# A transformer block on one core: the first feed-forward product by Strassen's seven half-sized products, one segment's output projection moved beside the feed-forward part, and phi finished on VectorE

## The chip, the cores and the metric

The kernel runs on 1 core of one Trainium2 chip. The metric is device time in microseconds (us), lower is better; a time is the median of several runs. TensorE (PE) does matrix products, VectorE (DVE) and ScalarE (ACT) elementwise work, GpSimd (POOL) selections and some elementwise work, and SyncE (SP) issues nearly every DMA.

## The reference

One block over 2048 tokens of 512 channels in float32: a modulated layernorm, an attention with a running memory in four segments of 512 tokens and 32 heads of 16 channels, an output projection, a second modulated layernorm, and a feed-forward part with squared ReLU.

```
phi = lambda t: where(t > 0, t + 1.0, exp(t))
for s in range(4):                                  # segments of 512 tokens
    a_dot = softmax(qs @ ks.T * scale + mask) @ vs
    a_mem = (phi(qs) @ M) / (phi(qs) @ z + 1e-6)
    o_s = g * a_mem + (1 - g) * a_dot
    M += phi(ks).T @ vs;  z += phi(ks).sum()
h = layernorm(x) * (1 + ca) + sa;   x = x + ga * (attention(h) @ wo)
h = layernorm(x) * (1 + cb) + sb;   x = x + gb * (relu(h @ w1 + b1)**2 @ w2 + b2)
```

Here w1 is 512 x 1792 and w2 is 1792 x 512. The change concerns `h @ w1`, phi, the two layernorms' reciprocal root, and the place of one quarter of `attention(h) @ wo`.

## The kernel before

**Precision.** Each large product is made of three float32r products: both operands are split into a high part and the rest, by a copy on ACT (high) and a subtraction on DVE or POOL (low), and high*high, high*low and low*high are added up in PSUM. So every operand of a product costs one ACT and one DVE or POOL instruction, and every product three matmuls.

**Attention.** It works in units: one unit is 8 heads of one segment (16 units, `u`). For a unit `qk` projects q and k channel-major into two PSUM banks, and L817 and L819 split them into `sg`, which DMAs (L835) scatter into the slots of `ST`. `a_quad` makes raw scores to find row maxima (L893, with DVE at L898), `b_quad` makes them again with the maximum subtracted (L1053), ACT takes the exponential (L1070), POOL zeroes the upper triangle (L1057), and L1112 multiplies by v (`bpv`). phi is built from the same banks: exp on ACT (L824), relu on ACT (L826), min(exp, 1) on POOL (L828) and the sum on POOL (L829). `heads_out` stores the raw result to DRAM, loads back denominators (L1171, L1173), forms the gates on DVE, stores and loads them spread out (L1192, L1195), multiplies on POOL (L1198) and stores the turned result (L1213).

**Output projection and second layernorm.** `wo_tile(g)` handles 128 tokens: load and split the attention result, 12 matmuls (L1244 to L1246, `bwop`), add x and take layernorm statistics on DVE. `ln2(s)` takes the reciprocal root for a segment in 11 small DVE instructions (L625 to L630), normalizes (L633), transposes on TensorE (L642, `blnq`), applies the modulation and splits the result into `H2a` (segments 0, 2) or the space of `WVO` (1, 3).

**Feed-forward part.** 14 slices `f` of 128 hidden channels. Weights are loaded and split once, while segment 0 is worked on, and stay. `ffn1(s, f)` makes 4 x 3 matmuls of 128x128 weights by 512 tokens (L1405 to L1407, `bh`). ACT adds the bias and clips (L1415) and squares into the high part (L1419), DVE squares again (L1422) and subtracts (L1423). `ffn2(s, f, t)` adds three matmuls (L1433 to L1435) to the output bank of each of the four 128-token tiles (`bpf`).

**What sets the order.** Every step is an `op` with an engine, an assumed duration, its predecessors, and the pool slots and PSUM banks it takes and gives back. A planner (`Plan.run`) walks the five engines in assumed time. On each engine it takes the steps in the order that the table `ORDER` lists by number, and emits them in that order. On the chip each engine is then a strict queue in that order; a step that must wait holds up everything behind it. The memory of the attention part (`sb`) is closed and given to the feed-forward weights at `open_ffn`; a tile there waits for the last use of what lay in its place.

## Time and profile before

| | |
|---|---|
| median of 3 runs | 799.09 us (796.88 to 800.13) |
| the profiled execution: its time | 797.94 us |
| the profiled execution: its span | 796.2 us |
| mean granted TensorE clock | 0.980 |
| instructions | 15771 |

The span runs from the first to the last instruction; 1.7 us of the execution's time lie around it. Roughly, the attention part lasts until 435 us, a change-over until 467 us, and the feed-forward part until the end. Busy shares add up the instructions' own times; matmuls are pipelined, so the distance between the starts of two neighbours, not their length, tells what one costs.

### The profile page before, as it was taken

How to read it: one execution, taken by the hardware profiler on the slowest of the kernel's cores; microseconds unless marked ns; L12 is line 12 of the kernel's file. 1: busy time of each engine (PE TensorE's matmuls, PEld its weight loads, DVE VectorE, ACT ScalarE, POOL GpSimd, SP SyncE). 2: the span in 40 equal slices, each digit the busy share in tenths (PEclk: the TensorE clock that was granted, in tenths of full speed). 3: DMA queues.
4: the chain of work that ended last, by engine and by line, in shares of the span. 5: the costliest groups of instructions: out<-in, count | busy, mean ns of one | idle time of the engine just before them, and what ended most of it. 6: DMA issues, size and time to landing. Idle time of an engine off the chain costs nothing.

```text
span 796.2 us, 15771 instructions
## 1 busy us (share of the span) xinstructions
PE 761.8 (96%) x5623; PEld 568.0 (71%) x5627; DVE 502.4 (63%) x1353; ACT 439.5 (55%) x931; POOL 277.4 (35%) x362
## 2 busy tenths in 40 slices
...
GB/s 258 199 152 95 239 186 175 116 126 159 194 174 167 168 196 165 174 154 194 201 224 220 109 216 118 93 67 27 0 1 1 1 76 4 1 0 80 1 0 54
DMA packets 76568, 95.29 MB, mean 120 GB/s; under 512 B 17349, under 2 KB 36553, under 8 KB 76490
## 3 DMA queue, kind: packets, MB, share of 16 engines
...
q8 instruction: 45, 0.74, 0.4%
...
q10 hardware_dynamic: 152, 0.13, 0.0%
...
## 4 chain that ended last, share of the span: by engine, by line
PE 73%; DMA 7%; ACT 6%; DVE 5%; SPq 5%; POOL 2%; issue 2%; ACTq 0%; DVEq 0%; POOLq 0%
PE bh L1407 7%; PE bh L1405 7%; PE bh L1406 7%; PE bpf L1434 7%; PE bpf L1433 6%; PE bpf L1435 6%; PE bpv L1112 6%; PE bqk L780 5%; PE bv L860 4%; PE bpb L1053 4%; PE ba L893 4%; ACT pt L1070 3%; SPq L835 3%; PE blnq L642 2%; PE bwarm L546 2%
## 5 line engine op out<-in xcount | busy, mean ns | idle before, releaser
L898 DVE CUSTOM_DVE_ANT_0 ba<-ba,msk 128x128 f32<-128x128 f32 (+2 forms) x384 | 186.5, 543 | 57.2 <-PE ba L893 44.6
L1070 ACT ACTIVATE pt<-bpb 128x512 f32<-128x512 f32 x320 | 171.5, 615 | 19.6 <-PE bpb L1053 17.2
L1422 DVE TENSOR_TENSOR r<-r 128x512 f32<-128x512 f32 x56 | 38.7, 692 | 136.8 <-ACT rr L1419 136.6
L780 PE MATMUL bqk<-HT,WQK 64*128 64x512 f32 x720 | 101.9, 399 | 0.2 <-POOL hinge_s L510 0.2
L1415 ACT ACTIVATE r<-bh,b1c 128x512 f32<-128x512 f32 x56 | 38.6, 689 | 109.5 <-PE bh L1407 65.0
L1057 POOL TENSOR_SCALAR_AFFINE_SELECT pt<-pt 128x512 f32<-128x512 f32 x128 | 79.9, 644 | 39.7 <-ACT pt L1070 31.8
L1434 PE MATMUL bpf<-W,rr 128*128 128x512 f32 x224 | 88.1, 393 | 0.0
L1433 PE MATMUL bpf<-W,rr 128*128 128x512 f32 x224 | 88.1, 393 | 0.0
L1435 PE MATMUL bpf<-W,rr 128*128 128x512 f32 x224 | 87.6, 391 | 0.0
L1112 PE MATMUL bpv<-pt,VT 128*32 128x512 f32 (+3 forms) x1024 | 81.5, 446 | 3.7 <-DVE mx L898 2.9
L1053 PE MATMUL bpb<-ST 64*128 64x256 f32 (+2 forms) x512 | 80.3, 353 | 3.1 <-ACT ac L931 1.2
L893 PE MATMUL ba<-ST 63*128 63x256 f32 (+2 forms) x512 | 78.0, 351 | 1.6 <-ACT phi L826 0.7
L780 PEld LDWEIGHTS bqk<-HT,WQK 64*128 64x128 f32 x720 | 71.6, 187 | 10.2 <-POOL hinge_s L510 0.9
L1419 ACT ACTIVATE rr<-r 128x512 fp32r<-128x512 f32 x56 | 35.4, 632 | 69.9 <-PE bpf L1435 65.7
L1053 PEld LDWEIGHTS bpb<-ST 64*128 64x128 f32 x512 | 51.1, 185 | 26.3 <-ACT pt L1070 6.7
L893 PEld LDWEIGHTS ba<-ST 63*128 63x128 f32 x512 | 51.7, 186 | 25.1 <-ACT pt L1070 7.3
L1198 POOL TENSOR_TENSOR X1L<-X1L 128x512 f32<-128x512 f32 x40 | 51.6, 1294 | 20.8 <-DMA X1L<-o_gate 18.9
L1112 PEld LDWEIGHTS bpv<-pt,VT 128*32 128x32 f32 x1024 | 29.1, 110 | 37.9 <-issue 26.4
L898 DVE DVE_READ_ACCUMULATOR2_ANT mx<- 128x1 f32 x384 | 54.1, 141 | 0.1
L860 PE MATMUL bv<-WVO,HT 64*128 64x512 f32 x384 | 53.8, 395 | 0.0
L1405 PE MATMUL bh<-H2a,W 128*128 128x512 f32 x112 | 45.5, 406 | 6.3 <-ACT W L1373 6.3
L1433 PEld LDWEIGHTS bpf<-W,rr 128*128 128x128 f32 x224 | 42.1, 188 | 9.8
(157 smaller groups left out, 1433.7 us busy)
## 6 DMA issues: line engine op xcount, KB each, us to landing
...
```

The costliest lines, as they stand in the source:

```text
L780: m = nc.tensor.matmul(bank(("qk", u, w)), W3(w, k, x, cc * P, (cc + 1) * P)[z], HT[z, y, k], start=(ph == 0 and k == 0 and i == 0), stop= ...
L860: m = nc.tensor.matmul(bank(("v", s, t)), HT[z, x, k, t * P:(t + 1) * P], WVO[z, k, y], start=(ph == 0 and k == 0 and i == 0), stop=(ph == ...
L893: nc.tensor.matmul(dst[:, c0:c0 + n], ST[b:b + 63, 0, sl, qt * P:(qt + 1) * P], ST[b:b + 63, 1, sl, :n], start=True, stop=True)
L898: nc.vector.tensor_tensor_reduce(i, i, msk[:, 512 - n:], scale=1.0, scalar=-3e38, op0=ALU.add, op1=ALU.max, accum_out=o)
L1053: nc.tensor.matmul(dst, ST[b:b + 64, 1, sl, kb * P:(kb + 1) * P], ST[b:b + 64, 0, sl, q0:512], start=True, stop=True)
L1057: nc.gpsimd.affine_select(out=ap, in_=ap, pattern=[[0, ap.shape[1]], [1, P]], compare_op=ALU.is_ge, fill=0.0, base=0, channel_multiplier=-1)
L1070: ns = [act(512, lambda j=j: nc.scalar.activation(buf("PPP"[n], pt)[:, i + j], bank(keys[j]), AF.Exp, scale=0.25), pr[slot] + 0.01 + 0.001 ...
L1112: nc.tensor.matmul(bank(o)[32 * hq:32 * hq + 32, q0:q0 + src.shape[1]], v[:, a:a + 32], src, start=start, stop=stop, tile_position=(0, 32 ...
L1405: nc.tensor.matmul(p, wh, h2[:, 0, k], start=(k == 0), stop=False)
L1433: nc.tensor.matmul(p, rh, FF["W2"][:, f, 0], start=(f == 0), stop=False)
L1434: nc.tensor.matmul(p, rh, FF["W2"][:, f, 1], start=False, stop=False)
L1435: nc.tensor.matmul(p, rl, FF["W2"][:, f, 0], start=False, stop=(f == NF - 1))
```

## The change

**ffn1.** The token axis of a segment is cut in two halves of 256, the contraction in two halves of 2 x 128 channels, and the hidden channels in pairs of slices (`q`, seven per segment). A 2x2 block product then needs 8 half-sized products; a Strassen-type scheme needs seven. `ln2` forms seven combinations of the normalized activations (four subtractions) and splits each; `load_w1` forms seven combinations of the weights (four additions) and splits them. Per pair `q`, TensorE makes 7 products of 2 x 3 matmuls, each 256 wide, into two banks (`bhx`, `bhy`), and DVE adds them up into the four blocks of the hidden layer (L1504, L1507). Then ACT clips twice, squares, and copies the high part, all four blocks together, and DVE subtracts (L1533). The combined weights of all slices don't fit, so `load_w1(s, q)` loads and combines them again for every segment, in two buffers. Sums x1 of segments 0 to 2 are kept in DRAM (`x1_dram`) and loaded back.

**Output projection.** `wo_tile` of segment 2 joins segment 3's beside the feed-forward part; its low parts go from POOL to DVE.

**phi.** ACT's relu and POOL's sum become one DVE instruction that takes max(., 0) of the PSUM bank and adds min(exp, 1).

**Layernorm.** The reciprocal root becomes two POOL instructions, an addition and a power. In the first layernorm of segments 1 to 3, half of the modulation goes from ACT to DVE.

`ORDER` is another table. Its effect at three places follows. TensorE around the last score-times-value product (`bpv`, the end of attention), before:

```order
L1246 MATMUL bwop<-WVO,oT 128x512
L1112 MATMUL bpv<-pt,VT_139 32x512 x4
L1112 MATMUL bpv<-pt,VT_139 32x384 x4
L1112 MATMUL bpv<-pt,VT_139 32x128 x4
L1112 MATMUL bpv<-pt,VT_139 32x256 x4
L642 MATMUL blnq<-ident,xh 128x128 x8
L1244 MATMUL bwop<-WVO,oT 128x512
```

and changed:

```order
L650 MATMUL blnq<-ident,x_6398 128x128 x4
L650 MATMUL blnq<-ident,x_6453 128x128 x4
L650 MATMUL blnq<-ident,x_6902 128x128 x4
L650 MATMUL blnq<-ident,x_6664 128x128 x4
L1119 MATMUL bpv<-pt,VT_142 32x512 x4
L1119 MATMUL bpv<-pt,VT_142 32x384 x4
L1119 MATMUL bpv<-pt,VT_142 32x128 x4
L1119 MATMUL bpv<-pt,VT_142 32x256 x4
L1260 MATMUL bwop<-WVO,oT 128x512
```

All transposes of segment 0's second layernorm now stand ahead of the last `bpv`. Behind it stood 16 transposes and 36 matmuls of `bwop` before the first `bh`; now 21 of `bwop` stand there before the first `bhx`: the rest of segment 1's last tile and nine matmuls of segment 2's first. Ahead of it stand 84 matmuls of `bwop`, where there were 108.

SP at the same place, before (the last unit's denominators, gates, and then the feed-forward weights `wr`):

```order
L1263 DMA xw<-in_A_x 128x512
L1171 DMA den<-o_raw_79 128x1x32
L1173 DMA den<-o_raw_79 128x1x32
L1179 DMA X1L<-o_raw_79 128x1x512
L1213 DMA o_turned_63<-X1L 128x512
L1263 DMA xw<-in_A_x 128x512
L1192 DMA o_gate_95<-den 128x2x32
L1176 DMA X1L<-o_raw_79 128x1x512
L1195 DMA X1L<-o_gate_95 128x1x512 x2
L1371 DMA wr<-in_B_w 128x4x128
```

and changed (`x_dram_61` is `x1_dram` of segment 1, `w1r` the raw weights of a pair of slices):

```order
L1306 DMA x_dram_61<-x_7083 128x512
L1183 DMA X1L<-o_raw_82 128x1x512
L1178 DMA den<-o_raw_82 128x1x32
L1180 DMA den<-o_raw_82 128x1x32
L1276 DMA ot<-o_turned_65 128x4x128
L1434 DMA w1r<-in_B_w 128x4x128 x2
L1276 DMA ot<-o_turned_65 128x4x128
L1434 DMA w1r<-in_B_w 128x4x128 x2
L1417 DMA gbb<-gb_dram 128x512
L1459 DMA wr<-in_B_w 128x512
L1276 DMA ot<-o_turned_65 128x4x128
L1199 DMA o_gate_98<-den 128x2x32
```

The first weights now stand ahead of the last unit's gate store, not behind it, but behind the store of the last x1 tile of segment 1.

DVE in the middle of the feed-forward part of segment 0, before (`r`, `rr` the hidden layer of one slice, `W_7273` the first weights' low part):

```order
L1422 TENSOR_TENSOR r<-r 128x512
L1423 TENSOR_TENSOR rr<-r,rr 128x512
L1374 TENSOR_TENSOR W_7273<-wr,W_7273 128x512
L1438 TENSOR_TENSOR X_6093<-X_6093,gab 128x512
L664 TENSOR_TENSOR WVO<-xh,WVO 128x2x256 x2
L656 TENSOR_SCALAR xh<-blnq,modc 128x256
L1422 TENSOR_TENSOR r<-r 128x512
```

and changed, the larger part of one pair `q`:

```order
L1507 TENSOR_TENSOR u<-u,bhx 128x256
L664 TENSOR_SCALAR xh<-blnq,modc 128x256
L1504 TENSOR_TENSOR r<-bhy,u 128x2x256
L1507 TENSOR_TENSOR r<-r,bhy 128x256
L1443 TENSOR_TENSOR w1d<-w1r,w1d 128x1024
L1507 TENSOR_TENSOR r<-u,bhx 128x256
L1460 TENSOR_TENSOR wr<-wr,gbb 128x512
L664 TENSOR_SCALAR xh<-blnq,modc 128x256
L1462 TENSOR_TENSOR W_7114<-wr,W_7114 128x512
L1322 TENSOR_TENSOR WVO<-xh,WVO 128x512
L1507 TENSOR_TENSOR r<-r,bhy 128x2x256
L1443 TENSOR_TENSOR w1d<-w1r,w1d 128x768
```

Before, one slice takes two 512-wide instructions of DVE, and the weights' split once in the program. Changed, a pair takes twelve: six on the weights (the third is L1448, four sums), six on the hidden layer. From the first L1443 on DVE has 486 instructions.

The diff, cut to its core:

```diff
+    mhalf = const.tile([P, 4], F32)
+    MHN = op("POOL", 0.1, lambda: nc.gpsimd.memset(mhalf, -0.5), -5.0)
     def ln_rstd(mvs, n):
-        v = small.tile([P, n], F32, name="lnv")
-        y = small.tile([P, n], F32, name="lny")
-        t = small.tile([P, n], F32, name="lnt")
         var = mvs[:, :, 1]
-        nc.vector.tensor_scalar(v, var, EPS_LN, None, op0=ALU.add)
-        nc.vector.tensor_scalar(y.bitcast(I32), v.bitcast(I32), -0.5, float(0x5F3759DF), op0=ALU.mult, op1=ALU.add)
-        for it in range(3):
-            nc.vector.scalar_tensor_tensor(t, y, -0.5, y, op0=ALU.mult, op1=ALU.mult)
-            nc.vector.tensor_tensor(t, t, v, op=ALU.mult)
-            nc.vector.scalar_tensor_tensor(var if it == 2 else y, t, 1.5, y, op0=ALU.add, op1=ALU.mult)
+        nc.gpsimd.tensor_scalar(var, var, EPS_LN, None, op0=ALU.add)
+        nc.gpsimd.tensor_tensor(var, var, mhalf[:, :n], op=ALU.pow)
...
-            if low == "POOL":
-                af = [op("ACT", 0.9, lambda f=affine: f("av"), pr + 0.01 + 0.001 * j, after=[*n, *MODC[sc]], put=[b[j]])]
-            else:
-                af = [op("ACT", 0.46, lambda f=affine: f("a"), pr + 0.01 + 0.001 * j, after=[*n, *MODC[sc]], put=[b[j]]),
-                      op("DVE", 0.46, lambda f=affine: f("v"), pr + 0.01 + 0.001 * j, after=[*n, *MODC[sc]], put=[b[j]])]
+            af = [op("ACT", 0.46, lambda f=affine: f("a"), pr + 0.01 + 0.001 * j, after=[*n, *MODC[sc]], put=[b[j]]),
+                  op("DVE", 0.46, lambda f=affine: f("v"), pr + 0.01 + 0.001 * j, after=[*n, *MODC[sc]], put=[b[j]])]
+            if bare:
+                out.append(af)
+                continue
...
                 x1_ = act(512, lambda b=b, e=e: nc.scalar.activation(buf("e", e), bank(b), AF.Exp), p2 + 0.001, after=[hi],
-                          get=[("e", e)], put=[b])
-                x2_ = act(512, lambda b=b, f=f, w=w: nc.scalar.activation(buf(f"phi{w}", f), bank(b), AF.Relu), p2 + 0.002,
-                          after=[hi], get=[(f"phi{w}", f)], put=[b])
+                          get=[("e", e)])
                 m_ = op("POOL", 1.44, lambda e=e: nc.gpsimd.tensor_scalar(TL[e], TL[e], 1.0, None, op0=ALU.min), p2 + 0.002, after=[x1_])
-                PHN[u, w] = op("POOL", 1.23, lambda e=e, f=f: nc.gpsimd.tensor_tensor(TL[f], TL[f], TL[e], op=ALU.add), p2 + 0.003,
-                               after=[m_, x2_], put=[e])
+                PHN[u, w] = dve(512, lambda b=b, e=e, f=f, w=w: nc.vector.scalar_tensor_tensor(
+                    buf(f"phi{w}", f), bank(b), 0.0, TL[e], op0=ALU.max, op1=ALU.add), p2 + 0.003, after=[m_, lo], get=[(f"phi{w}", f)],
+                    put=[e, b])
...
     def wo_tile(g, pr):
...
+        beside = s >= NS - 2
+        pool = "rr" if beside else "oT"
...
-        free = [N_FFN if last else N_LATE]
+        free = [N_FFN] if last else [N_LATE, *(x for l in H2N[0] for x in l)] if beside else [N_LATE]
...
+        if not last:
+            X1D[g] = sp(lambda: nc.sync.dma_start(x1_dram[s][(g % 4) * P:(g % 4 + 1) * P, :], x1(g)), pr + 0.055, 1 << 18, lat=1.3,
+                        after=[n], put=keep)
...
     def ln2(s, pr, wait=()):
...
+        def split(n, i, j, b):
+            v = lambda: tl(i, j).rearrange("p (k n) -> p k n", k=2)
+            h = act(512, lambda: nc.scalar.copy(h2(s, b)[:, 0], v()), pr[2] + 0.02, sbuf=True, after=[*n, *wait])
+            lo = op("DVE", 0.6, lambda: nc.vector.tensor_tensor(h2(s, b)[:, 1], v(), h2(s, b)[:, 0].bitcast(F32), op=ALU.subtract),
+                    pr[2] + 0.03, after=[h], put=[kk(i, j)] if b > 2 else ())
+            H2N[s][b] = [h, lo]
+            return [lo]
...
+        t1 = sub((0, 0), (1, 0), (0, 0), l00 + F[1][0])
+        t3 = sub((1, 0), (1, 1), (1, 0), [t1] + F[1][1])
+        t2 = sub((1, 1), (1, 1), (0, 0), [t1, t3] + l11)
+        t4 = sub((0, 1), (0, 1), (1, 1), [t2] + l10)
+        split([t1], 0, 0, 3)
+        split([t2], 1, 1, 4)
+        split([t3], 1, 0, 5)
+        split([t4], 0, 1, 6)
...
-    for s in range(NS - 1):
+    for s in range(NS - 2):
...
+    def load_w1(s, q, pr):
+        kr, kd = ("w1r", s, q), ("w1d", s, q)
+        def load():
+            TL[kr] = FF["sb"].tile([P, 4, 2, P], F32, name="w1r", tag=f"w1r{PL.slot[kr]}")
+            for h in (0, 1):
+                f = 2 * q + h
+                nc.sync.dma_start(TL[kr][:, 2 * h:2 * h + 2].rearrange("p a k n -> p (a k) n"),
+                                  w1[:, f * P:(f + 1) * P].rearrange("(k p) n -> p k n", p=P))
+        def hi(a, b, o):
+            if kd not in TL:
+                TL[kd] = FF["sb"].tile([P, 2, 7, 2, P], F32R, name="w1d", tag=f"w1d{PL.slot[kd]}")
+            nc.scalar.copy(TL[kd][:, 0, o:o + b - a], TL[kr][:, a:b])
+        def lo(a, b, o):
+            nc.vector.tensor_tensor(TL[kd][:, 1, o:o + b - a], TL[kr][:, a:b], TL[kd][:, 0, o:o + b - a].bitcast(F32), op=ALU.subtract)
+        def sums():
+            r = TL[kr]
+            for o, a, b, f in ((1, 0, 1, ALU.add), (0, 2, 0, ALU.subtract), (2, 1, 2, ALU.subtract), (3, 3, 2, ALU.subtract)):
+                nc.vector.tensor_tensor(r[:, o], r[:, a], r[:, b], op=f)
+        n = sp(load, pr - 0.2, 1 << 19, 2, after=[N_FFN], get=[("w1r", kr)])
+        h = act(768, lambda: hi(1, 4, 0), pr, sbuf=True, after=[n], get=[("w1d", kd)])
+        l = dve(768, lambda: lo(1, 4, 0), pr + 0.01, after=[h])
+        n = op("DVE", 1.36, sums, pr + 0.02, after=[l])
+        h2_ = act(1024, lambda: hi(0, 4, 3), pr + 0.03, sbuf=True, after=[n])
+        l2_ = dve(1024, lambda: lo(0, 4, 3), pr + 0.04, after=[h2_], put=[kr])
+        W1N[s, q] = ([h, l], [h2_, l2_])
...
+    def ffn1(s, q, pr):
+        x, y, kd = ("hx", s, q), ("hy", s, q), ("w1d", s, q)
+        r, rr, u = ("r", s, q), ("rr", s, q), ("u", s, q)
+        wa, wb = W1N[s, q]
+        B = H2N[s]
+        def mm(a, b, key, c):
+            w, m, p = TL[kd], h2(s, b), bank(key)[:, 256 * c:256 * c + 256]
+            for k in (0, 1):
+                nc.tensor.matmul(p, w[:, 0, a, k], m[:, 0, k], start=k == 0, stop=False)
+                nc.tensor.matmul(p, w[:, 0, a, k], m[:, 1, k], start=False, stop=False)
+                nc.tensor.matmul(p, w[:, 1, a, k], m[:, 0, k], start=False, stop=k == 1)
+        def prod(i, key, c, pr, after, **kw):
+            a, b = {1: (1, 0), 2: (2, 1), 3: (6, 2), 4: (0, 6), 5: (4, 3), 6: (5, 4), 7: (3, 5)}[i]
+            return pe("F", 0.712, lambda: mm(a, b, key, c), pr + 0.001 * i, after=[*(wa if a < 3 else wb), *B[b], *after], **kw)
+        rt = lambda: TL[r]
+        two = lambda t: t.rearrange("p (c n) -> p c n", c=2)
+        def u1():
+            TL[u] = FF["sb"].tile([P, 2, 256], F32, name="u", tag=f"u{PL.slot[u]}")
+            nc.scalar.copy(TL[u][:, 0], bank(x)[:, :256])
+        def u34():
+            TL[r] = FF["sb"].tile([P, 4, 256], F32, name="r", tag=f"r{PL.slot[r]}")
+            nc.vector.tensor_tensor(rt()[:, 0:4:3], two(bank(y)), TL[u][:, 1:2, :].to_broadcast([P, 2, 256]), op=ALU.add)
+        def add(o, a, b):
+            return lambda: nc.vector.tensor_tensor(o(), a(), b(), op=ALU.add)
+        p1 = prod(1, x, 0, pr, [], get=[("#D", x)])
+        n1 = act(256, u1, pr + 0.001, after=[p1], get=[("u", u)])
+        p6 = prod(6, x, 1, pr + 0.01, [p1])
+        n2 = dve(256, add(lambda: TL[u][:, 1], lambda: TL[u][:, 0], lambda: bank(x)[:, 256:]), pr + 0.011, after=[p6, n1])
+        p7 = prod(7, y, 0, pr + 0.02, [p6], get=[("#D", y)])
+        p5 = prod(5, y, 1, pr + 0.03, [p7])
+        n3 = dve(512, u34, pr + 0.031, after=[p5, n2], get=[("r", r)])
+        n4 = dve(256, add(lambda: rt()[:, 1], lambda: rt()[:, 0], lambda: bank(y)[:, 256:]), pr + 0.032, after=[n3])
+        p2 = prod(2, x, 0, pr + 0.04, [p5, n1, n2])
+        n5 = dve(256, add(lambda: rt()[:, 2], lambda: TL[u][:, 0], lambda: bank(x)[:, :256]), pr + 0.041, after=[p2, n3], put=[x, u])
+        p4 = prod(4, y, 0, pr + 0.05, [p2, n4])
+        p3 = prod(3, y, 1, pr + 0.06, [p4], put=[kd])
+        F1[s, q] = p3
+        n6 = dve(512, add(lambda: rt()[:, 0:4:3], lambda: rt()[:, 0:4:3], lambda: two(bank(y))), pr + 0.061, after=[p3, n4], put=[y])
+        def relu(i):
+            nc.scalar.activation(rt()[:, 2 * i:2 * i + 2], rt()[:, 2 * i:2 * i + 2], AF.Relu, bias=b1c[:, 2 * q + i:2 * q + i + 1])
+        a = [act(512, lambda i=i: relu(i), pr + 0.062 + 0.001 * i, sbuf=True, sc=1, after=[n6, n4, n5, n_b1]) for i in (0, 1)]
+        def high():
+            TL[rr] = FF["sb"].tile([P, 2, 4, 256], F32R, name="rr", tag=f"rr{PL.slot[rr]}")
+            nc.scalar.copy(TL[rr][:, 0], rt())
+        n = act(1024, lambda: nc.scalar.activation(rt(), rt(), AF.Square), pr + 0.064, sbuf=True, after=a)
+        h = act(1024, high, pr + 0.065, sbuf=True, after=[n], get=[("rr", rr)])
+        n = dve(1024, lambda: nc.vector.tensor_tensor(TL[rr][:, 1], rt(), TL[rr][:, 0].bitcast(F32), op=ALU.subtract), pr + 0.066,
+                after=[h], put=[r])
+        return [h, n]
...
```

More of the change, by code (lines that the diff above doesn't have):

```diff
@@ L398, in block_kernel @@
     dram = ctx.enter_context(tc.tile_pool(name="dram", bufs=1, space=bass.MemoryType.DRAM))
+    x1_dram = [dram.tile([L, D], F32, name=f"x1_dram{s}") for s in range(NS - 1)]
     o_turned = [dram.tile([D, L], F32, name=f"o_turned{s}") for s in range(NS)]
@@ L702, in ln1 @@
                 st[t].left += 1
-        r = op("DVE", 2.16, lambda: ln_rstd(TL[mv], 4), p_stat + 0.05, after=st)
+        r = op("POOL", 0.5, lambda: ln_rstd(TL[mv], 4), p_stat + 0.05, after=[*st, MHN])
         HTN[s] = []
```

441 lines of the change are left out of this document (232 added, 209 removed), and 15 rows, old and new, of the table ORDER.

## The prediction

> **What bounds the kernel now.** I read the page's engine line first, then busy time by stage, then the single matmuls of the feed-forward part, last the change-over between the parts.
>
> ```profile
> PE 761.8 (96%) x5623; PEld 568.0 (71%) x5627; DVE 502.4 (63%) x1353; ACT 439.5 (55%) x931; POOL 277.4 (35%) x362
> ...
> 150.00:250.00 100.00, 98.27 (x1108) 71.09 (x1106) 79.69 (x273) 89.35 (x212) 69.30 (x94) 1.00 0.56 157
> 250.00:350.00 100.00, 98.22 (x1054) 67.56 (x1051) 78.34 (x262) 83.24 (x195) 69.83 (x94) 1.00 0.61 168
> 350.00:435.00 85.00, 82.19 (x686) 49.63 (x684) 65.87 (x186) 61.80 (x133) 57.32 (x68) 0.98 0.72 206
> 435.00:467.00 32.00, 18.89 (x64) 14.39 (x65) 20.67 (x40) 6.91 (x12) 9.52 (x8) 0.74 0.55 150
> 467.00:792.00 325.00, 325.00 (x1428) 263.76 (x1428) 152.72 (x270) 103.19 (x166) 0.00 (x0) 1.00 0.12 38
> ```
>
> The stage rows give start and end, length, then busy time of PE, PE's weight loads, DVE, ACT and POOL, the granted clock, the DMA share and GB/s. From 467 us on TensorE is busy without a gap at full clock, DVE 47% and ACT 32% of the time: here only TensorE's work counts, and what is taken from it is won. From 435 to 467 us TensorE is busy 18.9 of 32 us at a mean clock of 0.74: this stage waits. Before 435 us everything is loaded, TensorE at 97 to 98%, ACT at up to 89%, DVE at 80%.
>
> **ffn1: the price of a 256-wide matmul.** The kernel has that shape once, in the first unit's projections (48 matmuls of 128x128 weights by 256 columns; the columns are start, length, engine, line):
>
> ```profile
> 25.88 0.28 PE L771 MATMUL bqk<-HT,WQK 128*128 128x256 f32 x1
> 25.88 0.19 PEld L772 LDWEIGHTS bqk<-HT,WQK 128*128 128x128 f32 x1
> 31.39 0.28 PE L772 MATMUL bqk<-HT,WQK 128*128 128x256 f32 x1
> ...
> 602.97 0.40 PE L1405 MATMUL bh<-WVO,W 128*128 128x512 f32 x1
> 605.78 0.40 PE L1433 MATMUL bpf<-W,rr 128*128 128x512 f32 x1
> ```
>
> The first and third rows are the second and the last of the 48: 5.51 us over 46 steps, 0.120 us each. The last two rows enclose twelve matmuls of ffn1: 2.81 us, 0.234 each. A pair of slices costs 24 x 0.234 = 5.62 us now and 42 x 0.120 = 5.03 us after. Over 28 pairs that is 157.4 against 140.9: **-16.5 us**, all of it on the path that sets the end.
>
> Each of the 256-wide matmuls follows a weight load that lasts 0.19 us, longer than the 0.120 us between starts, so the loads overlap. [...]
>
> **The change-over.** TensorE's idle times in it, with the SP rows that precede the first weights and the chain's piece for their transfer:
>
> ```profile
> 432.19 2.67 PE L1112 MATMUL bpv<-pt,VT 128*32 128x512 f32 x32
> 440.82 1.97 PE L642 MATMUL blnq<-ident,xh 128*128 128x128 f32 x8 [5.96 <-DVE xh L633]
> 450.83 0.66 PE L642 MATMUL blnq<-ident,xh 128*128 128x128 f32 x4 [0.75 <-DVE xh L633]
> 461.25 0.79 PE L1405 MATMUL bh<-H2a,W 128*128 128x512 f32 x1 [6.25 <-ACT W L1373]
> 467.19 0.46 PE L1405 MATMUL bh<-H2a,W 128*128 128x512 f32 x1
> ...
> 436.01 0.42 SPq L1259 DMA_DIRECT2D ot<-o_turned  x1
> 445.82 0.35 SPq L1263 DMA_DIRECT2D xw<-in_A_x  x1
> 446.21 0.60 SPq L1171 DMA_DIRECT2D den<-o_raw  x1
> 455.85 0.59 SPq L1371 DMA_DIRECT2D wr<-in_B_w  x1
> ...
> 455.85 4.64 DMA wr<-in_B_w
> 567.96 0.87 PE blnq L642 x8
> ```
>
> From the last bpv's end (434.86) to 467.19 pass 32.3 us. The work in them at full clock is 16 transposes (2 x 0.87), 36 bwop and 12 bh at 0.234: 13.0 us. So **19.3 us are lost** to waits and to half clock after them. Three queues cause it: layernorm's DVE chain ahead of blnq; SP, stuck at xw for 9.8 us ahead of the last unit's denominators; and the weights behind the last gates.
>
> In the changed order the transposes stand ahead of the last bpv, the reciprocal root on POOL, and the weights ahead of the gates. Counted from the last bpv's end, TensorE first has the rest of segment 1's last tile, 12 x 0.234 = 2.8 us. Then DVE's add (0.7), and on SP the x1 store (0.4), one load of o_raw (0.5), two denominators (0.6 each), one ot (0.4) and the weights (0.6 for the first half, the same for the second) bring the transfer to about 7 us; it lands 4.6 us later, and ACT and DVE split it (0.7 and 0.9, scaled by width): the first bhx at about 13. The nine matmuls of segment 2 fill 2 us of this. I take 8 us idle, 3 at half clock (from 461.25 to 467.19 twelve matmuls took 5.9 instead of 2.8), and 1 until the second set of weights, whose sums DVE makes only then: 12 lost where 19.3 were. **-7 us**; at best -14 (only the transfer stays), at worst 0, if DVE is late for the add on which SP waits.
>
> DVE has some ten two-operand instructions of the activations' combinations there, beside six POOL products for the gates. A neighbour costs it:
>
> ```profile
> 433.86 1.28 POOL L1276 TENSOR_TENSOR oT<-ot,oT 128x512 fp32r<-128x512 f32 x1
> 433.94 1.22 DVE L630 SCALAR_TENSOR_TENSOR lny<-lnt,lny 128x4 f32<-128x4 f32 x1
> 435.58 0.17 DVE L630 SCALAR_TENSOR_TENSOR lny<-lnt,lny 128x4 f32<-128x4 f32 x1
> ```
>
> The same instruction takes 1.22 us beside POOL and 0.17 alone. If all six collide, 6 x 1.28 = 7.7 us use up the gain; that is the worst case just named.
>
> The 24 bwop matmuls that leave the attention part (5.6 us) return in the feed-forward part at the same price: nothing, as long as TensorE had no spare time where they stood.
>
> **phi and the layernorms, in the attention part.**
>
> ```profile
> L826 ACT ACTIVATE phi<-bqk 128x512 f32<-128x512 f32 x24 | 15.1, 629 | 0.7 <-DVE sg L819 0.7
> L829 POOL TENSOR_TENSOR phi<-phi,e 128x512 f32<-128x512 f32 x24 | 31.4, 1308 | 1.5 <-ACT phi L826 0.8
> L819 DVE TENSOR_TENSOR sg<-bqk,sg 128x512 fp32r<-128x512 f32 x32 | 21.5, 687 | 14.8 <-ACT sg L817 9.5 <-DMA o_gate<-den 2.0 <-ACT e L824 1.6
> L828 POOL TENSOR_SCALAR e<-e 128x512 f32<-128x512 f32 x24 | 35.9, 1494 | 9.9 <-ACT e L824 7.8 <-issue 2.0
> ```
>
> ACT loses 15.1 us, POOL 31.4. DVE gains 24 instructions that the trace doesn't show; nearest is L819, also one PSUM and one SBUF operand, 0.69: 16.5 us (at worst double). The bank is held through POOL's min (1.5 us) where ACT's relu had freed it. The modulation moves 12 instructions from ACT to DVE; the roots leave it. POOL's power isn't in the trace either: between nothing and the 1.5 us of L828, off TensorE's path. The fullest engine gets room, DVE rises from 80% to some 84%. I take **-2 us**, from -8 to +6.
>
> **DVE beside the feed-forward part.**
>
> ```profile
> 522.03 0.68 DVE L1382 TENSOR_TENSOR W<-wr,W 128x512 fp32r<-128x512 f32 x1
> 522.63 0.99 DVE L656 TENSOR_SCALAR xh<-blnq,modc 128x256 f32<-128x256 f32 x2
> 524.13 0.69 DVE L1422 TENSOR_TENSOR r<-r 128x512 f32<-128x512 f32 x1
> 524.86 0.69 DVE L1423 TENSOR_TENSOR rr<-r,rr 128x512 fp32r<-128x512 f32 x1
> 788.45 0.76 DVE L1443 TENSOR_TENSOR X1L<-bpf,X1L 128x256 f32<-128x256 f32 x2 [1.19 <-PE bpf L1435]
> ```
>
> Back to back a 512-wide instruction costs 0.60 us (first to second row); one that needs the last one's result 0.73 (third to fourth). Two 256-wide ones take 0.76, so a column costs about 1 ns and an instruction 0.09. A pair now needs twelve instructions with 5632 columns: 6.7 us, beside TensorE's 5.03 + 24 x 0.234 = 10.6. Over a later segment that is 47, with layernorm and combinations (10) and sums (5) 62 us beside 76. In segment 0 the second weights (28 x 0.60 = 17) and eight bwop tiles (1.9 each, 15) come on top: 94 beside 74 + 87 bwop x 0.234 = 94. There the two run level, and any wait of DVE stops TensorE. All 486 instructions priced so make 269 us beside TensorE's 324 (141 + 157 for ffn2, which has as many matmuls as ffn1 now, 20 for bwop, 5 for transposes). I take **+5 us**, almost all in segment 0; 0 to 22.
>
> The weights of all segments add about 11 MB, the sums' way through DRAM 8 MB, over 325 us in which DMA now moves 38 GB/s: +58 GB/s, hidden under the 150 and more of the earlier stages; if not, a pair waits for its weights.
>
> **The sum.** -16.5 - 7 - 2 + 5 = -20.5. The profiled execution took 797.94 us (span 796.2), 1.15 below the median: **777 us**.
>
> **Rivals.**
> *VectorE becomes the bound* (slower). Place: DVE's queue from the first bhx on. Each of the 486 instructions would cost the dependent price, 0.12 us more: 58 us, so 327 beside TensorE's 324; with about 1 us per pair waiting for TensorE and ACT (28), 355. My forecast has 324 + 5 there, so this is +26: 803 us. It decides once a DVE instruction costs over 0.1 us more than back to back. For it: the recombination is a chain, and its strided and broadcast forms aren't in the trace. Against: neighbours in the queue mostly belong to different chains, and only some five per pair follow directly.
> *The change-over and the attention part don't gain*: 0 and +6 instead of -7 and -2, with DVE at +10: 797.94 - 16.5 + 6 + 10 = 797, no change that shows.
> [...]
>
> **The numbers.** Forecast 0.73 with its own range 764 to 790; the no-gain rival 0.11; VectorE 0.13; weight loads 0.01; the rest, 0.02, is a better change-over and attention part than I can see, down to 797.94 - 16.5 - 14 - 8 = 759. 0.5% is 4 us, what a measurement tells from no change. Faster 0.76, same 0.10, slower 0.14. The range is 759 to 800: it leaves out the slower rival.
>
> **What would show it.** Right: starts of bhx 0.12 us apart; under 14 us lost between the last bpv and steady work; DVE at 80 to 85% busy behind it. Wrong: TensorE idle behind DVE (L1504, L1507, L1533) for over 15 us in sum, bhx waiting for w1d in later segments, or the last bpv no earlier than now.

## The result, and the profile after

The changed kernel takes **774.96 us** (median of 4 runs, 772.39 to 778.96); the kernel before took 799.61 us beside it (796.88 to 801.37). The ratio is 0.970, with a 95% interval of 0.965 to 0.975. The forecast was 777, with a range of 759 to 800.

The profiled execution took 775.37 us (span 773.7), 22.6 less than the 797.94 of before. The page's engine line:

```profile
PE 744.4 (96%) x6128; PEld 581.0 (75%) x6131; DVE 632.9 (82%) x1543; ACT 501.8 (65%) x977; POOL 255.4 (33%) x351
```

The stages, as in the prediction (start and end, length, busy time of PE, PE's weight loads, DVE, ACT, POOL, granted clock, DMA share, GB/s):

```profile
150.00:250.00 100.00, 99.22 (x1094) 71.38 (x1084) 83.90 (x270) 82.96 (x196) 60.42 (x89) 1.00 0.59 162
250.00:350.00 100.00, 98.52 (x1050) 69.35 (x1048) 80.27 (x262) 79.38 (x184) 61.84 (x88) 1.00 0.64 173
430.00:460.00 30.00, 19.90 (x107) 17.11 (x108) 26.78 (x44) 12.79 (x19) 6.78 (x6) 0.83 0.87 240
460.00:560.00 100.00, 98.18 (x594) 86.24 (x593) 98.03 (x170) 59.07 (x86) 1.27 (x2) 1.00 0.45 135
560.00:774.00 214.00, 209.38 (x1295) 187.01 (x1293) 171.01 (x287) 113.40 (x151) 1.92 (x2) 1.00 0.24 71
```

TensorE is as full as before, with less to do. DVE, 47% busy in the feed-forward part before, is now full beside segment 0 (98 of 100 us) and at 80% behind it.

TensorE's rows at the change-over and inside a pair (start, length, engine, line, output from inputs; in brackets the idle time before, and what ended it):

```profile
423.72 2.36 PE L1119 MATMUL bpv<-pt,VT 128*32 128x512 f32 x32
428.69 0.39 PE L1262 MATMUL bwop<-WVO,oT 128*128 128x512 f32 x1
438.63 0.79 PE L1260 MATMUL bwop<-WVO,oT 128*128 128x512 f32 x1 [9.55 <-ACT oT L1292]
442.51 0.28 PE L1487 MATMUL bhx<-H2a,w1d 128*128 128x256 f32 x1
453.26 0.39 PE L1487 MATMUL bhy<-H2a,w1d 128*128 128x256 f32 x1 [1.46 <-DVE r L1507]
699.76 0.28 PE L1487 MATMUL bhx<-WVO,w1d 128*128 128x256 f32 x1
700.72 0.28 PE L1489 MATMUL bhx<-WVO,w1d 128*128 128x256 f32 x1
```

SP's queue there:

```profile
430.44 0.32 SPq L1220 DMA_DIRECT2D o_turned<-X1L  x1
434.38 0.46 SPq L1276 DMA_DIRECT2D ot<-o_turned  x1
434.94 1.00 SPq L1434 DMA_DIRECT2D w1r<-in_B_w  x2
```

And the transfer of the first weights as the chain of waits has it:

```profile
435.43 4.21 DMA w1r<-in_B_w
```

The last bpv ends at 426.08; the first bhx follows 16.4 us later (32.3 from the last bpv to steady work before). One idle time of 9.55 us makes most of the loss: SP stood at the store of unit 14's output (L1220), which waits for GpSimd's products, until 430.44, and attention output and weights stand behind it. Of the first block, the eight steps from the sixth row to the seventh take 0.96 us, 0.120 each.

**The account.** Lost time is time less the matmuls at their own pitch, the mean over neighbours in these two traces: 0.234 for bh, 0.230 for bpf, 0.121 for bhx and bhy. Behind the last bpv's end TensorE took 357.6 us for 338.2 of work before, and takes 344.1 for 327.4 now.

| term | forecast | measured | from |
|---|---|---|---|
| ffn1 | -16.5 | -14.3 | 672 x 0.2336 = 157.0; 1176 x 0.1213 = 142.7 |
| change-over | -7 | -7.7 | 19.4 lost; 11.7 now, until 12 us of work are done |
| attention part | -2 | -4.9 | last bpv 8.8 earlier, less 5.6 (24 bwop moved), plus 1.7 (transposes now in front) |
| DVE beside the feed-forward part | +5 | +5.0 | 16.7 lost in all behind the last bpv, less 11.7 |
| moved bwop and transposes, rounding | 0 | -0.7 | the rest |
| sum | -20.5 | -22.6 | |

The attention term is the least certain: in the profiled executions of ten kernels with the same attention part the last bpv ended between 424 and 430 us, and of the kernel before there is one.

### The profile page after: what moved, and what is told of

Its sections match the earlier page's. It is cut to its first block, busy times and chain, and to the rows that moved or that the text cites. A ratio compares the mean times of both kernels' runs of the same rounds, so it can differ in the third digit from the quotient of the medians.

```text
span 773.7 us, 17109 instructions
## 1 busy us (share of the span) xinstructions
PE 744.4 (96%) x6128; PEld 581.0 (75%) x6131; DVE 632.9 (82%) x1543; ACT 501.8 (65%) x977; POOL 255.4 (33%) x351
## 4 chain that ended last, share of the span: by engine, by line
PE 69%; DVE 12%; DMA 6%; ACT 5%; issue 3%; SPq 3%; POOL 1%; DVEq 0%; POOLq 0%; ACTq 0%
PE bqk L788 7%; PE bpv L1119 6%; PE bpf L1547 5%; PE bpf L1546 5%; PE bpf L1548 5%; PE bv L867 5%; PE bpb L1060 5%; PE ba L900 5%; PE bhy L1487 3%; PE bhy L1489 3%; PE bhy L1488 3%; PE bwarm L558 2%; PE bhx L1487 2%; ACT pt L1077 2%; PE bhx L1489 2%
## 5 line engine op out<-in xcount | busy, mean ns | idle before, releaser
L788 PE MATMUL bqk<-HT,WQK 64*128 64x512 f32 x720 | 99.8, 397 | 0.2 <-POOL hinge_s L522 0.2
L1440 ACT CAST w1d<-w1r 128x768 fp32r<-128x768 f32 (+1 forms) x56 | 52.7, 942 | 63.6 <-PE bhy L1489 52.1
L1546 PE MATMUL bpf<-W,rr 128*128 128x512 f32 x224 | 88.4, 394 | 0.0
L1060 PE MATMUL bpb<-ST 64*128 64x256 f32 (+2 forms) x512 | 80.2, 353 | 5.3 <-DMA ST<-mt 2.1
L900 PE MATMUL ba<-ST 63*128 63x256 f32 (+2 forms) x512 | 78.1, 354 | 0.6 <-DVE mx L905 0.4
L788 PEld LDWEIGHTS bqk<-HT,WQK 64*128 64x128 f32 x720 | 69.9, 185 | 10.3 <-POOL hinge_s L522 1.1
L1060 PEld LDWEIGHTS bpb<-ST 64*128 64x128 f32 x512 | 53.0, 187 | 28.5 <-DVE mx L905 5.2
L1443 DVE TENSOR_TENSOR w1d<-w1r,w1d 128x768 fp32r<-128x768 f32 (+1 forms) x56 | 60.7, 1086 | 4.2 <-ACT w1d L1440 4.1
L867 PE MATMUL bv<-WVO,HT 64*128 64x512 f32 x384 | 55.7, 398 | 0.2 <-POOL hinge_s L522 0.2
L1525 ACT ACTIVATE r<-r,b1c 128x512 f32<-128x512 f32 x56 | 38.4, 719 | 25.4 <-DVE r L1507 25.3
L637 POOL TENSOR_SCALAR st_all<-st_all 128x4 f32<-128x4 f32 x4 | 2.0, 504 | 153.9 <-DVE st_all L630 153.9
L1448 DVE TENSOR_TENSOR w1r<-w1r 128x256 f32<-128x256 f32 x112 | 47.5, 424 | 3.4
```

The source lines that it names most:

```text
L788: m = nc.tensor.matmul(bank(("qk", u, w)), W3(w, k, x, cc * P, (cc + 1) * P)[z], HT[z, y, k], start=(ph == 0 and k == 0 and i == 0), stop= ...
L867: m = nc.tensor.matmul(bank(("v", s, t)), HT[z, x, k, t * P:(t + 1) * P], WVO[z, k, y], start=(ph == 0 and k == 0 and i == 0), stop=(ph == ...
L900: nc.tensor.matmul(dst[:, c0:c0 + n], ST[b:b + 63, 0, sl, qt * P:(qt + 1) * P], ST[b:b + 63, 1, sl, :n], start=True, stop=True)
L1060: nc.tensor.matmul(dst, ST[b:b + 64, 1, sl, kb * P:(kb + 1) * P], ST[b:b + 64, 0, sl, q0:512], start=True, stop=True)
L1443: nc.vector.tensor_tensor(TL[kd][:, 1, o:o + b - a], TL[kr][:, a:b], TL[kd][:, 0, o:o + b - a].bitcast(F32), op=ALU.subtract)
L1546: nc.tensor.matmul(p, rh, FF["W2"][:, f, 0], start=(f == 0), stop=False)
```

## The experiments

Each kernel is the changed one with one edit. The intervals of the ratios are at most 0.5% to each side, 4 us; two of these kernels differ clearly by their medians from some 5 us on. Closer is the length of each stage in the profiled execution; segments that do the same agree within 0.2 us from kernel to kernel (78.1, 76.3, 88.4 below). A segment lasts from its first bhx to the next segment's, the last one to TensorE's last matmul.

| kernel | median | ratio to before | last bpv ends | to first bhx | seg 0 | seg 1 | seg 2 | seg 3 | bpv to end |
|---|---|---|---|---|---|---|---|---|---|
| changed kernel | 774.96 | 0.970 | 426.1 | 16.4 | 84.9 | 78.1 | 76.3 | 88.4 | 344.1 |
| two of three terms in ffn1 | 763.56 | 0.953 | 425.0 | 17.1 | 83.7 | 75.3 | 72.1 | 83.4 | 331.5 |
| eight products | 790.06 | 0.987 | 424.1 | 16.6 | 87.7 | 81.2 | 80.2 | 93.3 | 359.0 |
| no sums of the weights | 770.79 | 0.962 | 426.3 | 16.0 | 82.2 | 76.3 | 75.5 | 88.3 | 338.2 |
| low part twice (DVE) | 803.52 | 1.003 | 425.9 | 16.1 | 94.1 | 84.5 | 81.1 | 94.2 | 369.9 |
| high part twice (ACT) | 793.78 | 0.991 | 425.8 | 16.2 | 89.0 | 82.3 | 81.1 | 94.1 | 362.8 |
| phi back | 793.39 | 0.991 | 447.0 | 15.6 | 84.8 | 78.1 | 76.3 | 88.4 | 343.1 |
| min twice (GpSimd) | 795.30 | 0.994 | 445.7 | 17.7 | 83.9 | 78.1 | 76.3 | 88.4 | 344.4 |
| root back | 788.51 | 0.985 | 431.7 | 18.2 | 91.5 | 78.0 | 78.0 | 88.3 | 353.9 |
| weights ahead | 776.70 | 0.971 | 425.6 | 14.5 | 87.0 | 78.1 | 76.3 | 88.4 | 344.3 |
| weights first | 777.24 | 0.971 | 428.1 | 11.2 | 90.8 | 78.1 | 76.3 | 88.4 | 344.8 |
| weights first, no sums | 771.48 | 0.964 | 430.4 | 11.3 | 90.0 | 76.3 | 75.5 | 88.3 | 341.3 |
| weights first, products on GpSimd | 776.54 | 0.971 | 425.1 | 11.2 | 91.6 | 78.3 | 76.3 | 88.4 | 345.8 |

### What bounds the feed-forward part

**Less for TensorE.**

```
     nc.tensor.matmul(p, w[:, 0, a, k], m[:, 0, k], start=k == 0, stop=False)
-    nc.tensor.matmul(p, w[:, 0, a, k], m[:, 1, k], start=False, stop=False)
-    nc.tensor.matmul(p, w[:, 1, a, k], m[:, 0, k], start=False, stop=k == 1)
+    nc.tensor.matmul(p, w[:, 0, a, k], m[:, 1, k], start=False, stop=k == 1)
```

> The changed kernel without the third of the three terms (low part of the weights times high part of the activations) in all seven products: 14 of 42 matmuls of 256 columns per pair leave, 28 x 14 x 0.120 = 47 us of TensorE's work; the output lacks that term. Theory T (TensorE sets the time from the second segment on, VectorE only beside segment 0): segments 1 to 3 give 21 x 1.68 = 35 us, segment 0, where VectorE's work is as long as TensorE's, nearly nothing: about 740 us. Rival V (VectorE's queue sets the time of the whole feed-forward part): VectorE's work is unchanged, so at most 5 us are gained: 770.

Behind the last bpv 12.6 us were gained, of 47. Both theories miss: T by 23 us, V by 6 or more. Segment 3, where DVE is far from full, gives 5.0 of 11.8.

**More for TensorE.**

```
-   return pe("F", 0.712, lambda: mm(a, b, key, c), ...
+   return pe("F", 0.712, lambda: [mm(a, b, key, c) for _ in range(2 if i == 7 else 1)], ...
```

> The changed kernel with one of the seven products computed twice, so that a pair has eight, as many columns as without Strassen: 28 x 6 x 0.120 = 20.2 us more of TensorE's work, nothing more for any other engine. T: +20.2, less what hides in segment 0's idle time behind VectorE (at most 5): 790 to 795 us. V: 0 to 5 more, 775 to 780.

T's range: 790.06, and 14.9 us of 20.2 behind the last bpv. Of the 5.0 us that an eighth product adds to a segment, 2.8 to 4.9 are paid.

**Less for DVE.**

```
             for o, a, b, f in (...):
-                nc.vector.tensor_tensor(r[:, o], r[:, a], r[:, b], op=f)
+                pass
```

> The changed kernel without VectorE's four sums of the weights' blocks per pair (the products then use the raw blocks, so the feed-forward result is another): 28 x 4 x 0.44 = 49 us less of VectorE's work. T: only TensorE's idle time behind VectorE goes, about 5 us of segment 0, and 1 to 2 us in which the second weights come late in the change-over: 768 to 771 us. V: 20 us and more: below 755.

T again: 5.9 us, 2.7 in segment 0, 1.8 in segment 1, 0.8 in segment 2, 0.1 in segment 3. DVE does not set the time by the mass of its work.

**More for DVE.**

```
-        l2_ = dve(1024, lambda: lo(0, 4, 3), ...
+        l2_ = dve(1024, lambda: [lo(0, 4, 3) for _ in (0, 1)], ...
```

> The changed kernel with one 1024-wide subtraction of the weights' low part done twice per pair: 28 x 1.05 = 29 us more of VectorE's work. T: only segment 0 has no room for it: 7 x 1.05 = +7, 782 us. V: all of it, +29, 804 us.

V's figure: 25.8 us, of 29 added, came out at the end. But V is not the cause either: its price was DVE's full queue, and in the last segment DVE has room. Segments 2 and 3 of this kernel, columns as above:

```profile
620.56:701.63 81.07, 76.89 (x476) 67.85 (x475) 75.42 (x121) 43.89 (x59) 1.93 (x2) 1.00 0.24 69
701.63:795.86 94.23, 90.50 (x533) 78.69 (x531) 71.42 (x109) 40.50 (x52) 0.00 (x0) 1.00 0.17 53
```

In the last one DVE is busy 71.4 of 94.2 us, TensorE 90.5, and the 7.35 us added still cost 5.8. Neither engine is full. If a loop through both sets the time, work on a third engine in it must cost the same.

**More for ACT.** The second copy stands at L1532.

```
-        h = act(1024, high, pr + 0.065, ...
+        h = act(1024, lambda: (high(), nc.scalar.copy(TL[rr][:, 0], rt())), pr + 0.065, ...
```

> The changed kernel with ACT's copy of the squared slices to their high part done twice per pair: 28 x 1.05 = 29 us more on ACT, which is busy 46 to 62% of the feed-forward part; nothing more on TensorE or VectorE. Theory L (from one pair's r to the next, through the single r buffer, runs a loop L1504, L1507, products 4 and 3, L1507, relu, square, high, low that is hardly shorter than TensorE's 10.65 us per pair): 5 to 6 us per segment as with the doubled subtraction on VectorE, 793 to 800 us. Theory B (only the busy time of an engine counts, and VectorE's is the full one): nothing, 775 to 778.

Theory L's figure, at the lower end: 793.78, and 4.1, 4.2, 4.8 and 5.7 us in the four segments, though ACT is at most 67% busy. The chain that ended last, in this kernel's segment 3, shows the loop (start, duration, what):

```profile
716.47 1.06 ACT rr L1532
717.55 1.24 DVE rr L1533
718.88 0.70 DVE r L1504
719.61 0.43 DVE r L1507
720.08 0.38 PE bhy L1487
...
721.81 0.85 ACT w1d L1440
722.68 0.97 DVE w1d L1443
723.67 0.44 DVE w1r L1448
...
725.51 0.42 ACT w1d L1440
725.93 0.55 issue
726.48 1.05 ACT rr L1530
727.55 1.05 ACT rr L1532
728.63 1.23 DVE rr L1533
```

Read it from L1533 to L1533. The subtraction frees `r`, of which there is one buffer; L1504 and L1507 fill it and free the bank; products 4 and 3 end the use of `w1d`, of which there are two; ACT and DVE refill that, and in ACT's queue the next pair's high part stands behind the refill. So this round goes through the refill of `w1d`, where theory L had relu and square. Once round takes 11.08 us. In the changed kernel, one copy less, the same two rows of DVE are 10.19 us apart:

```profile
701.85 1.22 DVE L1533 TENSOR_TENSOR rr<-r,rr 128x1024 fp32r<-128x1024 f32 x1
712.04 1.22 DVE L1533 TENSOR_TENSOR rr<-r,rr 128x1024 fp32r<-128x1024 f32 x1
```

The round grew by 0.89 of the 1.06 us that the second copy takes. TensorE's share of a pair is 42 x 0.121 + 24 x 0.230 = 10.6 us on the mean, but single rounds of the changed kernel differ (9.2 to 12.7 us from the second segment on), so the margin between loop and TensorE can't be read from one of them. The segments give it. From segment 1 to segment 3, each kernel paid:

| added to each segment | paid in segments 1, 2, 3 | not paid, per pair |
|---|---|---|
| 7.4 us on ACT | 4.2, 4.8, 5.7 | 0.46, 0.37, 0.24 |
| 7.35 us on DVE | 6.4, 4.8, 5.8 | 0.14, 0.36, 0.22 |
| 5.0 us on TensorE | 3.1, 3.9, 4.9 | 0.27, 0.16, 0.02 |

**Less than 0.5 us per pair is free on any of the three engines**; the rest is paid. What is taken from one side uncovers the other: with a third of ffn1's matmuls gone, segment 2 takes 72.1 us, 10.3 per pair, although products 4 and 3, which lie on the loop, are four matmuls shorter there. And without the sums, which lie on the loop too, segment 3 gains only 0.1 us, since TensorE's work is left. In segment 0 the second subtraction cost 9.2 us, more than the 7.35 added: there DVE's own queue is full. The direct test, a second `r` buffer, was not made. So that this one loop carries all of the coupling is argued from the chain and the sizes, not shown by taking it away.

### The attention part

**phi back.**

```
-                PHN[u, w] = dve(512, lambda ...: nc.vector.scalar_tensor_tensor(
-                    buf(f"phi{w}", f), bank(b), 0.0, TL[e], op0=ALU.max, op1=ALU.add), ...
+                PHN[u, w] = dve(512, lambda ...: (nc.scalar.activation(buf(f"phi{w}", f), bank(b), AF.Relu),
+                    nc.gpsimd.tensor_tensor(TL[f], TL[f], TL[e], op=ALU.add)), ...
```

> The changed kernel with phi made as before, ACT's relu and GpSimd's add in place of the one instruction on VectorE, at the same place of the order: ACT gets 24 x 0.63 = 15 us back, GpSimd 24 x 1.31 = 31, VectorE loses 24 of about 0.7 = 17. If phi's move is what made the last bpv end earlier (8.8 us earlier, of which 3.7 are matmuls moved elsewhere): the last bpv ends about 4 us later than in the changed kernel, 779 us. If the roots on GpSimd or the order did: within 1 us, 775.

The last bpv came 20.9 us later and the kernel took 17 us more (0.991 against 0.970 of 800): the direction of the first case, four times its size. The edit puts work on ACT and on GpSimd; the next one separates them.

**GpSimd alone.** The second `min` stands at L836.

```
-   lambda ...: nc.vector.scalar_tensor_tensor(buf(f"phi{w}", f), bank(b), 0.0, TL[e], op0=ALU.max, op1=ALU.add)
+   lambda ...: (nc.vector.scalar_tensor_tensor(buf(f"phi{w}", f), bank(b), 0.0, TL[e], op0=ALU.max, op1=ALU.add),
+                nc.gpsimd.tensor_scalar(TL[e], TL[e], 1.0, None, op0=ALU.min))
```

> The changed kernel with GpSimd's min of phi done a second time behind VectorE's instruction (it changes nothing): 24 x 1.49 = 36 us more on GpSimd in the attention part, nothing more on ACT. With phi back on ACT and GpSimd the kernel took 17 us more. If GpSimd's queue is what cost them (the mask selections of L1064 stand behind phi's add): 12 to 20 us more, 788 to 795. If ACT's was: 0 to 3 more, 775 to 779.

GpSimd's queue it is: 19 us more, the last bpv 19.6 later, with nothing added on ACT. This kernel's waits for GpSimd and for phi from 50 to 440 us (total, times, longest; PEld are weight loads, PE the matmuls; L522 is a tiny GpSimd instruction that stands between the users of a bank):

```profile
PEld bpv L1119 <- POOL pt L1064: 14.1, 21, 1.9
PE bpv L1119 <- POOL pt L1064: 5.7, 6, 1.6
PE bv L867 <- POOL hinge_s L522: 5.2, 4, 1.9
POOL e L836 <- DVE phi L835: 8.6, 14, 1.4
```

One of its stages:

```profile
150.00:250.00 100.00, 96.01 (x1016) 65.39 (x1014) 79.39 (x253) 77.16 (x178) 66.51 (x87) 0.97 0.55 148
```

And the changed kernel's groups of phi and of the power:

```profile
L835 DVE SCALAR_TENSOR_TENSOR phi<-bqk,e 128x512 f32<-128x512 f32 x23 | 15.8, 685 | 3.5 <-POOL e L834 3.4
L638 POOL TENSOR_TENSOR mv<-mv,mhalf 128x4 f32<-128x4 f32 x2 | 2.1, 1047 | 0.2
```

GpSimd, busy two thirds of that stage, makes the weight loads wait 14.1 us for its mask selections (5.5 us in the changed kernel, 7.2 in the kernel before), and TensorE's matmuls stand 10.9 us for it, in the changed kernel for no GpSimd instruction over 0.2 us: in a strict queue each selection stands behind whatever was put ahead of it. DVE's phi instruction keeps its length (0.684 us for 0.686), so GpSimd does not cost time by slowing it. Not separated from the queue is the buffer `e`, which the second `min` holds longer: ACT's exp waits 6.8 us for it. Nor does the load alone decide: in the kernel before, GpSimd was busier in the same stage (69%) and TensorE busy 98%, so where the work stands in the order counts too. What phi's move alone would bring in the order of before is not shown; no such kernel was run.

**Root back.** Eleven small instructions, as before.

```
-        nc.gpsimd.tensor_scalar(var, var, EPS_LN, None, op0=ALU.add)
-        nc.gpsimd.tensor_tensor(var, var, mhalf[:, :n], op=ALU.pow)
+        nc.vector.tensor_scalar(v, var, EPS_LN, None, op0=ALU.add); nc.vector.tensor_scalar(y.bitcast(...), ...)
+        for it in range(3): nc.vector.scalar_tensor_tensor(t, y, ...); nc.vector.tensor_tensor(t, t, v, ...); nc.vector.scalar_tensor_tensor(...)
```

> The changed kernel with the layernorms' reciprocal root as before, a chain of eleven small instructions on VectorE, in place of two on GpSimd: about 2 us more in VectorE's queue at each of eight places. If the roots carried the attention part's gain: last bpv 3 to 5 us later, 779 us; in the feed-forward part three more chains hide, or cost a part of 2 us each. If phi did: 775 to 777.

The kernel took 788.51 us, 12 more by the ratios, where the first case had 779. The last bpv came 5.6 us later, as in that case, but the scatter named above is as large, so what the roots bring to the attention part stays open. Of the 9.8 us more behind the last bpv 6.6 lie in segment 0, 1.8 ahead of the first bhx and 1.7 in segment 2 (the other segments are 0.1 shorter each). Two roots follow each other in segment 0; the first and the last of their 22 instructions on DVE:

```profile
489.18 0.16 DVE L637 TENSOR_SCALAR lnv<-st_all 128x4 f32<-128x4 f32 x1
493.21 0.16 DVE L638 SCALAR_TENSOR_TENSOR st_all<-lnt,lny 128x4 f32<-128x4 f32 x1
```

TensorE's wait for them:

```profile
495.88 1.97 PE L650 MATMUL blnq<-ident,xh 128*128 128x128 f32 x8 [4.11 <-DVE xh L641]
```

And the ten microseconds from there on:

```profile
495.00:505.00 10.00, 9.12 (x37) 7.83 (x38) 8.49 (x17) 5.83 (x9) 0.00 (x0) 0.66 0.44 131
```

4.2 us of tiny instructions become 4.11 of idle TensorE, and then a granted clock of 0.66. My "hide, or cost a part of 2 us each" was wrong where DVE is full, and the prediction had let "the roots leave it" pass at no price.

### The change-over

**Weights ahead.** In SP's order (2424 is unit 14's store, 2646 the x1 store, 2816 the attention output's load, 2696 the first w1 load):

```
-2541 2635 2424 2544 2646 2543 2542 2816 2696 2794
+2541 2635 2646 2816 2696 2424 2544 2543 2542 2794
```

> The changed kernel with SP's order altered in one place: the x1 store of segment 1's last tile, segment 2's first attention output and the first w1 load stand ahead of the store that waits for unit 14's gates on GpSimd. Theory S (SP, stuck behind that store, holds up the change-over): the first weights land about 4 us earlier, the first bhx comes 2 to 3 us earlier (VectorE is busy with the activations' combinations until 436): 772 to 773 us. Rival: VectorE or the transfer itself sets it, less than 1 us: 775.

**Weights first.** The orders of SP, ACT and DVE (2818 and 2819 split the attention output, 2698 and 2699 are the first weights' low part and sums); the planner no longer asks for the last combinations and that tile's x1 before the memory changes over:

```
-2541 2635 2424 2544 2646 2543 2542 2816 2696 2794
+2541 2635 2816 2696 2646 2424 2544 2543 2542 2794
-2679 2669 2685 2687 2689 2691 2818 2697
+2679 2669 2818 2685 2687 2689 2691 2697
-2680 2683-2684 2686 2688 2690 2692 2645 2819 2545 2698-2699 2797
+2680 2683-2684 2819 2686 2688 2698-2699 2690 2692 2645 2545 2797
...
-        free = [N_FFN] if last else ...
+        free = [N_FFN] if last else [N_LATE] if g == 10 else ...
+    LATE += [x for l in H2N[0][3:] for x in l] + [X1N[6], X1D[6]]
```

> As the run before, with the attention output's and the weights' loads ahead of the x1 store too, and on ACT and VectorE the attention output's split and the first weights' low part and sums ahead of the last combinations of the activations. S: the first bwop of segment 2 at about 432 instead of 438.6, the first bhx at 436 instead of 442.5, and less half clock behind it: 5 to 6 us, 769 us. Rival (w1r's buffer comes free only when the last unit's outputs have left, or the products then wait for the combinations that were put back): 1 to 3 us, 772 to 774.

The first bhx came 1.9 and 5.2 us earlier behind the last bpv, somewhat less than S has it, and the whole gained nothing: 0.971 against 0.970, and 344.3 and 344.8 us behind the last bpv instead of 344.1. In the first kernel TensorE stands another 1.73 us within the first product, for the low part of the same weights on DVE (L1443). In the second one 6.4 us are lost by the first bhx, 11.6 in the changed kernel; by 10 us of work it is 11.9 and 11.6.

**Without the sums.** I put this down to DVE's full queue, and took the sums out of that kernel by the edit of "no sums".

> The kernel with the weights' loads first, and without VectorE's four sums of the weights' blocks (another feed-forward result). The first bhx came 5 us earlier there behind the last bpv (11.2 instead of 16.4), and segment 0 took 5.9 us longer. Theory D (from the last bpv to the end of segment 0 VectorE's queue sets the time and swallows the gain): with the sums gone the 4 to 5 us show against the changed kernel without sums (770.8): 766. Rival (half clock, transfers or the combinations put back swallow it): 770 to 772.

That theory fell. Against "no sums" nothing was gained: 771.48 us for 770.79, and from the last bpv to the end of segment 0 it took 101.3 us, against 98.2, with DVE busy 87 of them. TensorE's rows of this kernel name another engine:

```profile
445.18 0.50 PE L1260 MATMUL bwop<-WVO,oT 128*128 128x512 f32 x1 [1.44 <-ACT oT L1292]
450.47 0.39 PE L1487 MATMUL bhx<-H2a,w1d 128*128 128x256 f32 x1 [2.67 <-ACT w1d L1440]
```

In the kernel with the weights first, whose last bpv ends at 428.05, TensorE stands for the same two things, the attention output and the second pair's weights:

```profile
442.95 0.50 PE L1260 MATMUL bwop<-WVO,oT 128*128 128x512 f32 x1 [1.59 <-ACT oT L1292]
448.40 0.39 PE L1489 MATMUL bhx<-H2a,w1d 128*128 128x256 f32 x1 [0.72 <-DVE w1d L1443]
```

And SP's queue there:

```profile
433.52 0.52 SPq L1186 DMA_DIRECT2D X1L<-o_raw  x1
437.25 0.52 SPq L1183 DMA_DIRECT2D X1L<-o_raw  x1
439.61 1.05 SPq L1434 DMA_DIRECT2D w1r<-in_B_w  x2
```

Now the second tile's attention output and the second pair's weights are late. SP stands still from 434.04 to 437.25 ahead of unit 15's load; the profile names the postponed store, which must leave that load's buffer first (3.1 us). The second load of attention output and the second w1 load stand behind it; the latter is issued 11.6 us after the last bpv's end, where it was 10.5 (436.53 against 426.08). Of the 5.5 us lost between the first bhx and 10 us of work 2.5 are these waits, and most of the rest is a slower clock: 0.50 granted from 435 to 440 us, 0.84 from 440 to 445 and 0.78 from 445 to 450. So the first pair came earlier and the second did not: the stall on SP moved by one load. An order with both loads ahead was not tried.

**Products on GpSimd.** The kernel with the weights first, and in `load_w2` (L1460):

```
-        n = dve(512, lambda: nc.vector.tensor_tensor(wraw(k), wraw(k), FF["gbb"], op=ALU.mult), ...
+        n = dve(512, lambda: nc.gpsimd.tensor_tensor(wraw(k), wraw(k), FF["gbb"], op=ALU.mult), ...
```

> The kernel with the weights' loads first, and the product of the second weights' rows with the gate's row (L1460, 14 of 512 columns) on GpSimd instead of VectorE. VectorE loses 14 x 0.6 = 8.4 us between the last bpv and the end of segment 0, GpSimd gets 14 x 1.3 = 18 in a stage in which it has 8. Theory D: 5 to 8 us, 769 to 772. Rival (W2 comes late through GpSimd, or GpSimd slows VectorE beside it): no gain, 776 or more.

No gain, as the rival has it: 776.54 and 345.8 us behind the last bpv. The rival's reason is not shown; TensorE's longest waits there are again for the attention output (5.6 us in two) and for `w1d` (2.5 in three). No kernel here that computes the same beats the changed one.

## Why the prediction was right, and where its steps were off

**ffn1.** The price was read from 46 steps of the first unit; over the whole part the mean is 0.1213 and not 0.120, 2 us in 1176 matmuls. The weight loads overlap, as the rows said. No run shows the bound by weight loads to which the prediction gave a chance of 0.01: a load lasts 0.19 us, the matmuls start 0.1213 us apart, and eight products cost 14.9 us and not the 32 (168 x 0.19) that loads one behind the other would take.

**The change-over.** 7.7 us gained for a forecast of 7, with another cause in the middle. The forecast had SP free for seven DMAs behind the last bpv; SP stood at unit 14's store. Idle was 9.55 and not 8, half clock about 2 and not 3 (nine matmuls in 3.9 us instead of 2.1, at a granted clock of 0.52), and the second weights cost nothing. That the term fits so well is partly luck.

**The attention part.** -4.9 for -2 lies within the range (-8 to +6) and within the scatter of the last bpv. The reason was not the one the runs point to: I gave ACT, the fullest engine, as the one that is relieved. In the new order it is GpSimd's queue, at two thirds of its time, that TensorE waits for when work is added. Which part of the -4.9 comes from phi, the roots or the order stays open. Both unknown instructions came out as priced: phi's 0.685 us for 0.69, the power 1.05 us between nothing and 1.5.

**DVE beside the feed-forward part.** +5 was right in sum, but not in place. The forecast had almost all of it in segment 0, by DVE's queue; without the sums 2.7 us came back there and 2.7 in the later segments. The work was underestimated, 285 us from the first bhx on for 269. Most of that are the sums, of which the third needs the first, and the fourth the third:

```profile
707.97 1.81 DVE L1448 TENSOR_TENSOR w1r<-w1r 128x256 f32<-128x256 f32 x4
```

Four take 1.81 us; at 1 ns a column and 0.09 an instruction they were priced 1.38, and 28 x 0.43 = 12 us. The prediction's own row of two 256-wide instructions in 0.76 us would have given 1.52.

**The rival "VectorE becomes the bound".** It was set at "over 0.1 us more" per DVE instruction. The doubled subtraction adds 1.05 us to twelve instructions of a pair, 0.09 each, and cost 25.8 us. So the point of decision was about where I put it, and the kernel stood closer to it than a chance of 0.13 says. But behind segment 0 the mechanism is a loop through three engines and two buffers, not the length of DVE's queue, and ACT reaches it as well.

**The signs.** bhx 0.12 apart, 11.7 us lost before steady work, TensorE idle behind DVE for 3.9 us in all, no bhx waiting for w1d in later segments, the last bpv 8.8 us earlier: as forecast. DVE is busy 285 of 328 us, 87%, for 80 to 85.

So the forecast of 777 rests on one term whose working held, ffn1, and on three that came out near for reasons that were partly others; that the total is so close is partly luck.
